# Loading the query and key weights from the ACT and GpSimd queues in a fused attention and gated-MLP layer

## The chip, the cores and the metric

The kernel runs on one core of a Trainium2 chip. The metric is the device time of one execution in microseconds. A core has five engines with one instruction stream each: TensorE (PE in the profile; its weight loads are shown as PEld), VectorE (DVE), ScalarE (ACT), GpSimd (POOL) and SyncE (SP). A copy between the chip's memory (DRAM) and the core's on-chip memory (SBUF) is an instruction on SP, ACT or POOL that hands the copy to a queue; sixteen DMA engines then move the data and report its end through a semaphore. TensorE accumulates into banks of a second on-chip memory, PSUM.

## The reference

One layer on 2048 tokens of width 512: layer norm, sliding dilated attention with 32 heads of 16 channels and 8 keys per query at distances 0, 2, ..., 14, a residual, layer norm, a gated MLP of inner width 1376, a residual. All tensors are bfloat16.

```python
x = A_x                                                # 1 x 2048 x 512
h = x + _A_ref(_layernorm(x), A_wqkv, A_wo)
h2 = h + _B_ref(_layernorm(h), B_W_gate, B_W_up, B_W_down)

def _A_ref(x, wqkv, wo):
    q, k, v = split(x @ wqkv)                          # wqkv is 512 x 1536; 32 heads of 16
    idx = pos[:, None] - arange(8) * 2                 # masked where negative
    attn = softmax(where(mask, einsum(q, k[idx]) * 16 ** -0.5, -1e9))
    return einsum(attn, v[idx]).reshape(B, S, D) @ wo

def _B_ref(x, W_gate, W_up, W_down):
    return (relu(x @ W_gate) * (x @ W_up)) @ W_down
```

## The kernel before

The 2048 tokens are worked in four chunks of 512 (tk = 0 to 3), each of four blocks of 128 rows. For a chunk, DVE takes mean and variance of each block (L419, L422), ACT forms the reciprocal root (L432, L436), DVE normalizes the block into a tile `row` (L454), and TensorE transposes it with an identity matrix (L483; for some later blocks a DMA issued from SP does it, L472). The transposed block is copied into a tile `quad` by ACT (L499) or DVE (L497). TensorE then multiplies it by the query, key and value weights (L524), each result being four matmuls, one for each quarter `dt` of the 512 input channels; ACT evicts the result (L532). DVE forms query times shifted key (L571), TensorE sums it by head (L577), ACT takes the exponential (L593), DVE weighs the values (L659) and adds up (part of the adding is an accumulating DMA issued from POOL, L691), TensorE applies the output weight (L711), and after the second layer norm come gate and up (L749), their product on DVE (L769) and down (L786).

The order of the instructions on each engine is fixed when the kernel is built. A planner replays the operations by a table of ranks, and the code emits them in that order, so the main part is the same list whatever the loads do. Ahead of it stands `setup()`, emitted in source order, which the change touches. It holds, in this order:

- the four blocks of chunk 0 of x (128 KB each), alternately on SP and ACT (L282);
- the query and key columns of wqkv as four copies of 256 KB, one for each `dt`, into `wqk_sb` (L284);
- chunk 1 of x (512 KB) on SP (L285);
- a table load on ACT (L286) and a memset on DVE for the warm-up matmuls (L287);
- on POOL: the identity matrix (masks.py lines 197 and 199), the constant `eps_t` (L289), five iotas (L290 to L294; `ci` is the first) and two memsets (L295, L296);
- a one-element copy on POOL that reads x (L299), by which the load of the value weights on SP (L300) is held until a block of x is there; and another (L301), by which the loads of chunks 2 and 3 of x (L303) are held until chunk 1 is there. The loads of `wo`, `wu`, `wg` and `wd` follow on SP (L305 to L311);
- on DVE: the constants `tmp`, `cf`, `sel`, `spread`, `same` and `mask` (L316 to L324), made from the iotas. They stand ahead of the first layer norm on DVE's list.

TensorE starts with 44 warm-up matmuls of 128 columns (L373). After the transposes of the first two blocks of chunk 0 come two sets of eight more (L381). The first query and key results of chunk 0 are computed in halves: the first half needs only the first two blocks of x, but all four quarters of `wqk_sb`. TensorE's list then goes on in this order: that half result, the four transposes of a third block, the next half result, the transposes of the fourth block, more half results.

Of the kernel before, what the change touches and what calls it, by code (L numbers as in the profile page):

```python
# [187 lines left out]
def kernel(  # L188
# [11 lines left out]
    nc = tc.nc  # L200
    Bsz, S, D = A_x.shape
# [42 lines left out]
    wqk_sb = sb.tile([P, NT, 2 * D], BF16, name="wqk_sb")  # L244
# [33 lines left out]
    def setup():  # L278

        w3_r = A_wqkv.rearrange("(dt p) f -> p dt f", p=P)  # L280
        for j in range(BPC):
            (nc.scalar if j % 2 else nc.sync).dma_start(x_sm[:, j:j + 1, :], x_rows[:, j:j + 1, :])  # L282
        for dt in range(NT):
            (nc.scalar if dt % 2 else nc.sync).dma_start(wqk_sb[:, dt:dt + 1, :], w3_r[:, dt:dt + 1, 0:2 * D])  # L284
        nc.sync.dma_start(x_sm[:, BPC:2 * BPC, :], x_rows[:, BPC:2 * BPC, :])  # L285
        nc.scalar.preload_act_table_set("natural_log_exp_and_others")  # L286
        V.memset(warm[:], 0.0)  # L287
        make_identity(nc, identity[:])
        nc.gpsimd.memset(eps_t[:], EPS)  # L289
        nc.gpsimd.iota(ci[:], pattern=[[0, 1]], base=0, channel_multiplier=1)  # L290
        nc.gpsimd.iota(sel_i[:], pattern=[[1, H]], base=0, channel_multiplier=0)
        nc.gpsimd.iota(sp_i[:], pattern=[[1, H], [0, DQ]], base=0, channel_multiplier=0)
        nc.gpsimd.iota(sm_i, pattern=[[0, 4], [1, H]], base=0, channel_multiplier=0)
        nc.gpsimd.iota(mk_i[:], pattern=[[1, PADL]], base=0, channel_multiplier=0)  # L294
        nc.gpsimd.memset(kT[:, :, 0:PADL], 0.0)  # L295
        nc.gpsimd.memset(vT[:, :, 0:PADL], 0.0)  # L296


        nc.gpsimd.tensor_copy(out=wv_sb[0:1, 0, 0:1], in_=x_sm[0:1, 0, 0:1])  # L299
        nc.sync.dma_start(wv_sb[:], w3_r[:, :, 2 * D:3 * D])  # L300
        nc.gpsimd.tensor_copy(out=x_sm[0:1, 2 * BPC, 0:1], in_=x_sm[0:1, BPC, 0:1])  # L301
        for tk in range(2, NCK):
            nc.sync.dma_start(x_sm[:, tk * BPC:(tk + 1) * BPC, :], x_rows[:, tk * BPC:(tk + 1) * BPC, :])  # L303

        nc.sync.dma_start(wo_sb[:], A_wo.rearrange("(p t) f -> p t f", t=NT))  # L305
        nc.sync.dma_start(wu_sb[:], B_W_up.rearrange("(dt p) f -> p dt f", p=P))
        nc.sync.dma_start(wg_sb[:], B_W_gate.rearrange("(dt p) f -> p dt f", p=P))
        nc.sync.dma_start(
            wd_sb[:, 0:NFF, :], B_W_down[0:NFF * P, :].rearrange("(ft p) n -> p ft n", p=P))
        if FTAIL:  # L310
            nc.sync.dma_start(wd_sb[:FTAIL, NFF, :], B_W_down[NFF * P:F, :])  # L311


        for n, (op, by) in enumerate(((ALU.arith_shift_right, 2), (ALU.bitwise_and, H - 1),
                                      (ALU.arith_shift_right, 5))):
            V.tensor_scalar(out=tmp[:, n:n + 1], in0=ci[:], scalar1=by, scalar2=None, op0=op)  # L316
        V.tensor_copy(out=cf[:, 0:3], in_=tmp[:])
        V.tensor_scalar(out=cf[:, 2:3], in0=cf[:, 2:3], scalar1=1.0 * DIL, scalar2=None, op0=ALU.mult)
        V.tensor_scalar(out=cf[:, 3:4], in0=cf[:, 2:3], scalar1=4.0 * DIL, scalar2=None, op0=ALU.add)
        V.tensor_scalar(out=sel[:], in0=sel_i[:], scalar1=cf[:, 0:1], scalar2=None, op0=ALU.is_equal)  # L320
        V.tensor_scalar(out=spread[:], in0=sp_i[:], scalar1=cf[:, 1:2], scalar2=None, op0=ALU.is_equal)
        V.tensor_scalar(out=same[:], in0=sm_i, scalar1=cf[:, 1:2], scalar2=None, op0=ALU.is_equal)
        for hf in range(2):
            V.tensor_scalar(out=mask[:, hf, :], in0=mk_i[:], scalar1=cf[:, 2 + hf:3 + hf],  # L324
                            scalar2=None, op0=ALU.is_ge)
# [488 lines left out]
    with tc.manual_schedule():  # L814
        setup()
        for op in todo:
            if op.fn is not None:
                op.fn()
# [35 lines left out]
```

## Time and profile before

| | |
|---|---|
| median of four runs | 203.56 us (203.10 to 204.19) |
| the profiled execution | 204.76 us |
| its span in the trace | 203.0 us |
| TensorE busy | 193.6 us (95% of the span) |
| DVE busy | 153.3 us (76%) |
| ACT busy | 121.8 us (60%) |
| POOL busy | 12.7 us (6%) |

The profile covers one execution. "Span" is the time from the first to the last recorded instruction; the profiled execution's own time is 1.76 us longer. Times inside the trace count from the span's start. A row such as "7.94 0.41 PE L524 MATMUL ... x2" means: from 7.94 us on, 0.41 us long, two matmuls of line 524; text in square brackets says how long the engine was idle before and what ended that. The names ACTq, SPq and POOLq stand for the sequencers that issue DMAs.

### The profile page before, as it was taken

The page shows a single profiled execution, that of the slowest core. Times are in us where ns is not written, and L with a number is a line of the kernel's source. Part 1 is how long each engine was busy: PE and PEld are TensorE (multiplying, and loading weights), DVE is VectorE, ACT ScalarE, POOL GpSimd, SP SyncE. Part 2 cuts the span into 40 slices and gives each one's busy share as a digit, 9 for nine tenths or more (in the row PEclk, how much of TensorE's full clock was granted, in tenths as well). Part 3 has the DMA queues.
Part 4 walks back from the last instruction along what each step waited for, and adds up shares of the span by engine and source line. Part 5 has one row for each costly group of instructions (what it writes and reads, how often), then busy time and mean ns, then how long its engine had stood idle before and what let it go on. Part 6 is the DMA issues. An engine that isn't in the chain of part 4 may idle for free.

```text
span 203.0 us, 2938 instructions
## 1 busy us (share of the span) xinstructions
PE 193.6 (95%) x1095; PEld 96.1 (47%) x1115; DVE 153.3 (76%) x239; ACT 121.8 (60%) x256; POOL 12.7 (6%) x28
## 2 busy tenths in 40 slices
PE   8799999989999999999999999999999999999990
PEld 8576446545445434434444444444444444444460
DVE  6689998989999999999996768799968313023241
ACT  3367698746899966787436779601567521477300
POOL 3000000420000013100131000000000000000000
PEclk9999999999999999999999999999999999999999
DMA  5969952895000009920399400221010130200103
GB/s 146 345 203 393 399 181 53 149 204 111 3 0 0 0 3 171 196 46 3 57 178 193 118 3 0 46 58 52 3 52 0 26 78 3 78 0 0 52 0 107
DMA packets 17677, 18.83 MB, mean 93 GB/s; under 512 B 8352, under 2 KB 14464, under 8 KB 17664
## 3 DMA queue, kind: packets, MB, share of 16 engines
q1 hardware_dynamic: 15360, 11.57, 18.4%
q0 software_dynamic: 1728, 6.29, 16.5%
q10 hardware_dynamic: 576, 0.79, 1.4%
q8 instruction: 9, 0.15, 0.3%
q14 instruction: 4, 0.03, 0.0%
HBM read 8.42 MB, written 2.10 MB: 52 GB/s over the span
## 4 chain that ended last, share of the span: by engine, by line
PE 65%; DVE 15%; DMA 8%; ACT 5%; SPq 2%; issue 2%; ACTq 0%
PE bank L749 28%; PE bank L524 15%; PE bank L786 14%; DVE big L659 6%; PE bank L711 5%; DMA quad<-row 4%; DMA wqk_sb<-in_A_wqkv_dram 3%; DVE big L571 3%; DVE gT L769 2%; SPq L472 1%; DVE x_sm L722 1%; DVE big L662 1%; PE bank L577 1%; PE bank L483 1%; ACT big L644 1%
## 5 line engine op out<-in xcount | busy, mean ns | idle before, releaser
L749 PE MATMUL bank<-quad,wu_sb 128*128 128x512 bf16 (+1 forms) x172 | 42.3, 379 | 0.4
L749 PE MATMUL bank<-quad,wg_sb 128*128 128x512 bf16 (+1 forms) x173 | 42.0, 379 | 0.3 <-DMA quad<-row 0.3
L756 ACT ACTIVATE gr<-bank 128x512 bf16<-128x512 f32 (+1 forms) x44 | 25.4, 618 | 24.7 <-PE bank L749 22.9
L786 PE MATMUL bank<-wd_sb,gT 128*128 128x512 bf16 (+2 forms) x183 | 39.8, 366 | 0.2
L753 ACT CAST up_sb<-bank 128x512 bf16<-128x512 f32 (+1 forms) x44 | 25.1, 601 | 21.0 <-PE bank L749 17.3
L571 DVE TENSOR_TENSOR big<-quad,kT 128x4096 bf16<-128x4096 bf16 x16 | 36.2, 2285 | 0.2
L659 DVE TENSOR_TENSOR big<-big,vT 128x4096 bf16<-128x4096 bf16 x16 | 35.9, 2281 | 0.0
L769 DVE TENSOR_TENSOR gT<-gr,up_sb 128x1024 bf16<-128x1024 bf16 (+1 forms) x24 | 15.3, 642 | 24.0 <-ACT up_sb L753 14.4
L524 PE MATMUL bank<-quad,wqk_sb 128*128 128x512 bf16 (+1 forms) x139 | 30.2, 356 | 2.0 <-DMA wqk_sb<-in_A_wqkv_dram 0.9
L786 PEld LDWEIGHTS <-gT 128*128 128x128 bf16 (+1 forms) x187 | 18.1, 98 | 19.6 <-issue 0.4
L749 PEld LDWEIGHTS <-wg_sb 128*128 128x128 bf16 (+1 forms) x176 | 17.3, 100 | 21.2 <-issue 0.9
L749 PEld LDWEIGHTS <-wu_sb 128*128 128x128 bf16 (+1 forms) x176 | 17.5, 100 | 20.6 <-issue 0.7
L524 PEld LDWEIGHTS <-wqk_sb 128*128 128x128 bf16 x144 | 15.5, 114 | 14.1 <-issue 2.4
L797 DVE TENSOR_TENSOR row<-x_sm,bank 128x512 bf16<-128x512 bf16 (+1 forms) x17 | 10.6, 649 | 10.4 <-PE bank L786 10.4
L644 ACT CAST big<-bank 128x512 bf16<-128x512 f32 x32 | 17.8, 641 | 0.4 <-PE bank L638 0.2
L662 DVE TENSOR_TENSOR big<-big 128x1024 bf16<-128x1024 bf16 (+2 forms) x24 | 16.8, 728 | 0.1
L691 POOL DMA_DIRECT2D big<-big x12 | 10.5, 872 | 87.9 <-DVE big L659 59.9
L524 PE MATMUL bank<-quad,wv_sb 128*128 128x512 bf16 x62 | 15.6, 380 | 0.2
L711 PE MATMUL bank<-wo_sb,quad 128*128 128x512 bf16 x62 | 15.2, 379 | 0.2
L454 DVE TENSOR_SCALAR row<-x_sm,mv,rs 128x512 bf16<-128x512 bf16 x32 | 11.4, 407 | 3.7 <-ACT rs L436 3.1
L499 ACT COPY quad<-bank 128x1024 bf16<-128x1024 bf16 (+1 forms) x9 | 8.0, 931 | 7.2 <-PE bank L483 7.2
L532 ACT CAST quad<-bank 128x512 bf16<-128x512 f32 x16 | 9.5, 614 | 4.6 <-PE bank L524 4.6
(68 smaller groups left out, 147.2 us busy)
## 6 DMA issues: line engine op xcount, KB each, us to landing
big<-big POOLq DMA_DIRECT2D x12, 512.0 KB, 5.5
out_dram<-row SPq DMA_DIRECT2D x15, 128.0 KB, 1.8
x_sm<-in_A_x_dram SPq DMA_DIRECT2D x3, 512.0 KB, 5.3
wu_sb<-in_B_W_up_dram SPq DMA_DIRECT2D x1, 1376.0 KB, 9.4
wg_sb<-in_B_W_gate_dram SPq DMA_DIRECT2D x1, 1376.0 KB, 12.6
wd_sb<-in_B_W_down_dram SPq DMA_DIRECT2D x1, 1280.0 KB, 15.7
wqk_sb<-in_A_wqkv_dram ACTq DMA_DIRECT2D x2, 256.0 KB, 6.5
wqk_sb<-in_A_wqkv_dram SPq DMA_DIRECT2D x2, 256.0 KB, 6.6
```

Of the source, the lines that this page charges most:

```text
L454: V.tensor_scalar(out=xn.t[:], in0=x, scalar1=mv.t[:, j, 0:1], scalar2=rs.t[:, j:j + 1], op0=ALU.add if residual else ALU.subtract, op1=AL ...
L524: nc.tensor.matmul(mm.t[:, lo:hi], lhsT=wv_sb[:, dt, t:D:NT] if c == 2 else wqk_sb[:, dt, c * D + t:(c + 1) * D:NT], rhs=xnT.t[:, dt, lo:h ...
L571: V.tensor_tensor(out=pb.t[:].rearrange("p (t w) s -> p t w s", t=2), in0=q4, in1=k4, op=ALU.mult)
L644: nc.scalar.copy(out=ab.t[:, w, :], in_=bc.t[:])
L659: V.tensor_tensor(out=mt.t[:], in0=ab.t[:], in1=v8, op=ALU.mult)
L662: V.tensor_tensor(out=mt.t[:, 0:n, :], in0=mt.t[:, 0:n, :], in1=mt.t[:, n:2 * n, :], op=ALU.add)
L711: nc.tensor.matmul(od.t[:], lhsT=OT.t[:, t, j * P:(j + 1) * P], rhs=wo_sb[:, t, :], start=(t == 0), stop=(t == NT - 1 and tk not in RPE))
L749: nc.tensor.matmul(mm.t[:fs, :], lhsT=w_sb[:, dt, ft * P: ft * P + fs], rhs=hnT.t[:, dt, :], start=(dt == 0), stop=(dt == NT - 1))
L753: nc.scalar.copy(out=ub.t[:fs, i, :], in_=um.t[:fs, :])
L756: nc.scalar.activation(out=gr.t[:fs, i, :], in_=gm.t[:fs, :], func=ACT.Relu)
L769: V.tensor_tensor(out=gt.t[:fs, 0:n, :], in0=gr.t[:fs, 0:n, :], in1=ub.t[:fs, 0:n, :], op=ALU.mult)
L786: nc.tensor.matmul(od.t[:, c0:c1], lhsT=gts[ft].t[:fs, ft % 2, j * P:(j + 1) * P], rhs=wd_sb[:fs, ft, c0:c1], start=(ft == 0), stop=(ft == ...
```

## The change

The four copies of the query and key weights are given to other queues. Before, the quarters 0 and 2 were issued by SP and 1 and 3 by ACT; after, 0 and 1 are issued by ACT and 2 and 3 by POOL.

```diff
         for dt in range(NT):
-            (nc.scalar if dt % 2 else nc.sync).dma_start(wqk_sb[:, dt:dt + 1, :], w3_r[:, dt:dt + 1, 0:2 * D])
+            (nc.scalar if dt < 2 else nc.gpsimd).dma_start(wqk_sb[:, dt:dt + 1, :], w3_r[:, dt:dt + 1, 0:2 * D])
         nc.sync.dma_start(x_sm[:, BPC:2 * BPC, :], x_rows[:, BPC:2 * BPC, :])
```

In the built program the lists of TensorE, DVE and ACT have the same instructions in the same order as before. On POOL the two copies stand ahead of the identity matrix, so ahead of all of POOL's set-up but four constant memsets. On SP the copy of chunk 1 of x follows directly on the two blocks of chunk 0.

## The prediction

> **What bounds the kernel now.** I read the page first, then the chain of waits, then the timeline of the first 11 us, then who waits for whom. The busy table puts TensorE at 95% of the span, and its clock row shows full clock all along. Where TensorE waits at all decides what a moved load can do, so I went to the start of the chain of waits (start us, length us, what):
>
> ```profile
> 2.16 7.07 DMA wqk_sb<-in_A_wqkv_dram
> 9.23 0.05 issue
> 9.28 0.41 PE bank L524 x2
> 9.69 0.22 PE bank L483 x4
> 9.91 0.44 PE bank L524 x4
> ```
>
> The reader is to see that the first thing that holds TensorE is the last of the four q/k weight copies: issued at 2.16, there at 9.23. From there the chain runs through TensorE almost without a break to 32.55. The timeline says what stands around this wait:
>
> ```profile
> 0.74 0.20 POOL masks.py:197 MEMSET identity<- 128x128 bf16 x1 [0.29 <-POOLq L838]
> 1.30 0.13 POOL L290 IOTA ci<- 128x1 int32 x1
> 1.47 0.28 DVE L316 TENSOR_SCALAR tmp<-ci 128x1 int32<-128x1 int32 x3 [0.53 <-POOL ci L290]
> 2.83 0.37 DVE L324 TENSOR_SCALAR mask<-big,cf 128x16 bf16<-128x16 int32 x2
> 3.41 0.39 SPq L285 DMA_DIRECT2D x_sm<-in_A_x_dram  x1
> 3.62 0.69 DVE L419 BATCH_NORM_STATS2 st<-x_sm 128x6 f32<-128x512 bf16 x1 [0.42 <-DMA x_sm<-in_A_x_dram]
> ...
> 6.27 0.72 PE L483 MATMUL bank<-identity,row 128*128 128x128 bf16 x8 [0.45 <-DVE row L454]
> 7.34 0.39 DVE L497 COPY quad<-bank 128x512 bf16<-128x512 bf16 x1
> 7.94 0.41 PE L524 MATMUL bank<-quad,wqk_sb 128*128 128x256 bf16 x2
> 9.28 0.41 PE L524 MATMUL bank<-quad,wqk_sb 128*128 128x256 bf16 x2 [0.93 <-DMA wqk_sb<-in_A_wqkv_dram]
> ```
>
> Here is a second chain that runs beside the weights: POOL's iota `ci` feeds DVE's constants (1.47 to 3.20), these stand ahead of the first statistics on DVE (3.62), and the layer norm of two blocks is ready for TensorE when L497 ends, at 7.34 + 0.39 = 7.73. TensorE then does half of the first group and waits 0.93 us. So weights and layer norm are both early work with little room: the layer norm has some 1.5 us before TensorE would notice, and 0.42 us of that stands at DVE's wait for x.
>
> What a copy costs on POOL is shown only later, by the accumulating copies:
>
> ```profile
> 35.78 1.01 POOL L691 DMA_DIRECT2D big<-big  x1 [25.09 <-PE bank L524]
> 37.95 0.86 POOL L691 DMA_DIRECT2D big<-big  x1 [1.17 <-DVE big L659]
> ```
>
> and the page's queue table says in how many packets copies are cut:
>
> ```profile
> q0 software_dynamic: 1728, 6.29, 16.5%
> q10 hardware_dynamic: 576, 0.79, 1.4%
> ```
>
> q10 is ACT's queue (2 x 128 KB and 2 x 256 KB, 0.79 MB), 144 packets a copy; q0 is POOL's, 1728 / 12 = 144 a copy too. One packet per row and 16 more, so a q/k copy issued from POOL should take as long to describe as an L691.
>
> **What the Trainium skill says.** "DMA: Bandwidth & Descriptors", section "Issuing engines are not separate DMA queues", says that copies from all three engines run on the same sixteen DMA engines and that spreading saves only issue time. The trace agrees that issue is small: SP and ACT spend 0.92 and 0.94 us on two weight copies that need about 7. Its section "Queues, rings and completion order" says that each DMA engine takes packets from its queues in turn; the trace shows SP's and ACT's weight copies landing 6.6 and 6.5 us after issue (medians), which fits. "Perfetto Trace Analysis", section "DMA Instruction — SWDGE (GPSIMD)", says that POOL's row ends when the last descriptor is written; so 0.86 us is taken to be POOL's own time, though no POOL compute follows an L691 closely here. "TensorE: Matmul & The Clock Gate", Part 1, says that the clock halves after an idle window of about 3.4 us; no such drop is in this trace.
>
> **The change part by part.** (1) SP loses two issues of some 0.45 us and L285 its 0.8 us wait for x (SP's waits), so chunk 1 of x is issued at 1.68 instead of 3.41. Nobody is late for chunk 1: DVE reads it at 10.48 only. The value weights behind it (L300) wait for POOL, see (3). ACT still issues two copies: nothing.
>
> (2) POOL gains two issues ahead of everything. From the L691 rows, the first 1.01 and the second 0.86: 1.87, with a gap between them 1.9 us. Bounds: 1.0 if the second is overlapped with the first, 3.0 if a copy that POOL issues cold costs half as much again. Behind them stand the identity (now needed at 6.27, ready at 1.3, so 3.2 after), `eps_t` (needed 4.63) and `ci`. DVE's constants start at 1.47 + 1.9 = 3.37 and end at 5.1, so the first statistics start at about 5.0 instead of 3.62: 1.4 late (1.9 less 0.5, the wait for x and the overlap of two DVE instructions). All of the first layer norm moves with it: the first transposes 6.27 to 7.7, L497's end 7.73 to about 9.15. TensorE then does the whole first group at once, some 0.5 us (twice the 0.25 us from 9.28 to the next transposes at 9.53): transposes at 9.65 instead of 9.53. As far as POOL goes, TensorE is 0.1 late, because the layer norm slips into the time in which TensorE waited for weights. With POOL at 3.0 it would be 1.2, with 1.0 nothing.
>
> (3) L299 on POOL moves from 3.65 to about 4.3, so the value weights are issued 0.7 later; they took 7.9 us to land and TensorE first reads them at 17.38. L301 waits for chunk 1 (10.51), which comes no later. Both cost nothing; without that cover they would cost their 0.7 us.
>
> (4) The weights themselves. Bytes ahead of the last q/k packet: x 0.52 MB and q/k 1.05 MB. The stage table gives 275 GB/s at 2 to 3 us, 379 to 3.5, then only 119 and 102 to 4.5, 209 to 5, and 324 to 367 to 9: 1.9 MB by 8.7, so 0.3 to 0.4 MB of chunk 1 went between, on DMA engines that were done with their weights. After the change chunk 1 (1 KB rows) is on SP's queue beside weights (2 KB rows) on both others, and in turns. While ACT's 16 weight packets per DMA engine pass, so do 16 of chunk 1's. A 1 KB packet at 379 / 16 = 24 GB/s is an estimated 43 ns, so 0.7 us on the DMA engine that ends last. Against that, POOL's copies start early: L691's own landing is 5.5 us after issue, and POOL's first issue moves to 0.74, 0.9 ahead of the first weight issue now. Bounds for the last landing: 8.7 (early start wins) to 10.3 (chunk 1 between, and POOL's packets also hold back x). I take 9.75, that is +0.5.
>
> TensorE goes on when both are there; it is late by the larger of 0.1 and 0.5: **+0.5 us**.
>
> (5) Does it reach the end? DVE is busy without a gap worth naming from 13.84 to 32.3 and TensorE from 9.28 to 32.5; both hang on these first transposes. The later waits on transposes and weights are relative to that work, or loads that are early (traffic falls to 11 GB/s at 28 to 33). So it passes through whole. Profiled: span 203.0 to 203.5, own time 204.76 to 205.3. The median shown is 1.2 below the profiled time, so I put the difference on the median: 203.56 + 0.5 = **204.1**.
>
> **The rivals.** About 0.5%, 1.0 us, is what a measurement here can tell from no change.
>
> A, forecast: late by 0 to 1.0 us, weights or layer norm in each other's shadow. 204.1.
>
> B, slower: POOL's two issues become the bound. Place: `ci`, then DVE's constants, then all four blocks' statistics. Price: POOL's delay less 1.8 us. It passes 1.0 from a delay of 2.8 us, 1.4 per copy against the 0.86 shown. For: the early copies are the first that POOL issues, the first L691 is longer, and POOL's spans are rough. Against: the other eleven rows agree at 0.86. At 1.8 per copy: 3.6 - 1.8 = 1.8, giving 205.4. Weights that land past 10.3 go the same way.
>
> C, slower too: the clock. TensorE's gap between warm-up (ends 5.82) and the first transposes grows from 0.45 to 1.9 us. The warm-up at 4.83 us for 44 is 110 ns each, the 16 extra ones from 6.83 take 1.06 us, 66 each: full clock is won only shortly before the layer norm arrives. If it were lost for the window that the skill names, 3.4 us of work at half speed costs 1.7 us: 205.3. Against: some 1.4 us of matmuls still fall in that window.
>
> D, faster: POOL runs on after its issue and three queues bring the weights sooner, by 8.2. Then TensorE's 0.93 us wait goes: 202.6. For: the slack between 7.73 and 9.23 is real. Against: DVE's constants are behind POOL, and the same DMA engines carry it all.
>
> E: the copies change queue and nothing else moves; 203.6, inside A's range.
>
> **How the numbers follow.** A with E 0.46, B 0.30, C 0.13, D 0.11. Of D about a fifth (0.02) stays within the bound, and of A nothing leaves it. Faster 0.09, same 0.46 + 0.02 = 0.48, slower 0.30 + 0.13 = 0.43. B weighs as much as it does because its price rests on one kind of row seen late in the trace. The range takes A's lower part with the spread of medians, 203.2, and reaches over B and C to 205.7.
>
> **What would show it.** Right: POOL's rows L284 at 0.74, `ci` at about 3.2, DVE L316 at 3.4, the first statistics at 5.0, the first transposes at 7.7, the first L524 group without a gap inside it or with a short one at 9.7, and the chain of waits starting at a q/k copy on ACT's queue. Wrong: `ci` later than 4.3 (B), matmuls of 128 columns at 110 ns each after 9 us (C), an L524 group before 9.0 (D), or a new wait past 30 us, which I have argued away.

## The result and the profile after

The changed kernel takes 205.08 us (median of 30 runs, 203.93 to 208.84) against 203.59 us before (49 runs): a ratio of 1.0074, 95% interval 1.0058 to 1.0091. It is slower by about 1.5 us. Three of its 30 executions (207.44 to 208.84 us, granted clock 0.983) are left out of the ratio, which so rests on 27. The forecast was 204.1; 205.08 lies in the upper part of the range, and the loss of 1.5 us is on the side to which 0.43 had been given.

The spans alone hide this: 203.0 before, 203.2 after. The traces differ in the last microseconds, where stores land. Compared at the last DVE instruction, the loss is there. The timeline of the kernel before, then of the changed one (start us, us, engine, line, operation, idle before it):

```profile
198.32 0.42 DVE L797 TENSOR_TENSOR row<-x_sm,bank 128x256 bf16<-128x256 bf16 x1 [0.24 <-PE bank L786]
```

```profile
199.86 0.42 DVE L797 TENSOR_TENSOR row<-x_sm,bank 128x256 bf16<-128x256 bf16 x1 [0.24 <-PE bank L786]
```

That is 1.54 us later. What follows this row took 4.3 us in the first trace of the kernel before and 2.9 in the changed one; two further traces of the kernel before (b1, b2 below) have it at 198.39 and 198.41, with 3.1 us after it. The long tail of the first trace is not repeated there.

The head of the changed kernel's trace says where the 1.54 us come from. Its timeline:

```profile
1.28 1.28 POOL L284 DMA_DIRECT2D wqk_sb<-in_A_wqkv_dram  x2 [0.83 <-POOLq L838]
1.68 0.43 SPq L285 DMA_DIRECT2D x_sm<-in_A_x_dram  x1
3.13 0.13 POOL L290 IOTA ci<- 128x1 int32 x1
3.30 0.28 DVE L316 TENSOR_SCALAR tmp<-ci 128x1 int32<-128x1 int32 x3 [2.36 <-POOL ci L290]
4.93 0.68 DVE L419 BATCH_NORM_STATS2 st<-x_sm 128x6 f32<-128x512 bf16 x1
7.58 0.72 PE L483 MATMUL bank<-identity,row 128*128 128x128 bf16 x8 [2.17 <-DVE row L454]
8.13 1.84 PE L381 MATMUL bank<-warm 128*128 128x128 bf16 x16
8.64 0.39 DVE L497 COPY quad<-bank 128x512 bf16<-128x512 bf16 x1
9.76 1.16 PE L524 MATMUL bank<-quad,wqk_sb 128*128 128x256 bf16 x4
10.09 0.35 PEld L524 LDWEIGHTS <-wqk_sb 128*128 128x128 bf16 x3 [0.28 <-DMA wqk_sb<-in_A_wqkv_dram]
10.72 0.63 PE L483 MATMUL bank<-identity,row 128*128 128x128 bf16 x4
```

Three things are to be seen. POOL's two copies push `ci` from 1.30 to 3.13, and the layer norm follows: first transposes at 7.58 instead of 6.27. The 16 extra matmuls (L381) take 1.84 us where they took 1.06: TensorE is at half speed. And the weights' wait, seen here on TensorE's weight loads (PEld), now ends at 10.09 instead of 9.23. The third block's transposes start at 10.72 instead of 9.53, 1.19 late, and by the first full-width matmuls of L524 (13.57 against 11.94 in the chains of waits) it is 1.63.

The chain of waits says which of the three this execution was held by (pieces of it, start us, length us, what):

```profile
1.28 0.53 POOL wqk_sb L284
3.17 0.10 POOL ci L290
5.02 0.61 DVE st L419
7.58 0.72 PE bank L483 x8
8.30 1.68 PE bank L381 x16
9.97 0.95 PE bank L524 x4
```

It runs from POOL's issues through `ci`, DVE and the layer norm to the matmuls at half speed. No landing of a weight copy is in it: in this execution the weights are late behind work that is later still.

The table by stages gives the clock. Columns after the stretch: its length, busy us and instructions of PE, PEld, DVE, ACT and POOL, TensorE's granted clock, DMA share, GB/s:

```profile
5.40:7.60 2.20, 0.03 (x2) 0.03 (x2) 2.13 (x7) 1.00 (x4) 0.00 (x0) 1.00 0.93 322
7.60:8.20 0.60, 0.60 (x10) 0.50 (x11) 0.60 (x3) 0.23 (x2) 0.00 (x0) 1.00 1.02 371
8.20:10.00 1.80, 1.80 (x19) 1.61 (x16) 1.51 (x5) 1.06 (x5) 0.00 (x0) 0.50 0.81 289
10.00:11.60 1.60, 1.60 (x11) 1.20 (x11) 0.21 (x1) 0.00 (x0) 0.18 (x1) 0.50 0.26 90
11.60:13.00 1.40, 1.40 (x16) 1.38 (x15) 1.40 (x4) 0.58 (x1) 0.00 (x0) 0.99 0.67 200
```

TensorE is nearly idle from 5.4 to 7.6 and then has half its clock from 8.2 to 11.6. That is rival C of the prediction, come true.

### The profile page after: what moved, and what is told of

It reads as the page before. It is cut to its first block, busy times and chain, and to the rows that moved or that the text cites. A ratio compares the mean times of both kernels' runs of the same rounds, so it can differ in the third digit from the quotient of the medians.

```text
span 203.2 us, 2937 instructions
## 1 busy us (share of the span) xinstructions
PE 194.5 (96%) x1095; PEld 97.0 (48%) x1115; DVE 153.3 (75%) x239; ACT 121.8 (60%) x256; POOL 13.8 (7%) x30
## 3 DMA queue, kind: packets, MB, share of 16 engines
q0 software_dynamic: 1888, 6.82, 17.3%
## 4 chain that ended last, share of the span: by engine, by line
PE 70%; DVE 17%; ACT 7%; issue 2%; DMA 2%; POOL 1%; ACTq 0%; POOLq 0%
PE bank L749 28%; PE bank L524 18%; PE bank L786 14%; DVE big L659 6%; PE bank L711 5%; DVE big L571 3%; DMA quad<-row 2%; DVE gT L769 2%; PE bank L483 2%; DVE x_sm L722 1%; DVE big L662 1%; PE bank L577 1%; ACT big L644 1%; ACT kT L532 1%; ACT row L408 1%
## 5 line engine op out<-in xcount | busy, mean ns | idle before, releaser
L524 PE MATMUL bank<-quad,wqk_sb 128*128 128x512 bf16 (+1 forms) x139 | 30.7, 362 | 0.9 <-ACT lnd L613 0.7
L524 PEld LDWEIGHTS <-wqk_sb 128*128 128x128 bf16 x144 | 15.9, 115 | 12.9 <-issue 2.2
L524 PE MATMUL bank<-quad,wv_sb 128*128 128x512 bf16 x62 | 15.6, 380 | 0.2
```

Of the source, the lines that this page charges most:

```text
L524: nc.tensor.matmul(mm.t[:, lo:hi], lhsT=wv_sb[:, dt, t:D:NT] if c == 2 else wqk_sb[:, dt, c * D + t:(c + 1) * D:NT], rhs=xnT.t[:, dt, lo:h ...
```

## The experiments

Three causes are to be told apart: the layer norm that POOL delays (LN), the clock that is lost in the gap this opens (CLK), and the weights' later landing (W). Nine edited kernels were run, and the two kernels again. Ratios are to the kernel before as it was timed beside each experiment, with 95% intervals. Its median there was 203.16 us beside e1 to e4, 203.52 beside e5, e7, e9 and e9b, and 203.75 beside e8; differences of medians below are to these.

An execution's mean granted clock tells whether the clock was lost on the way. One stretch of 3.41 us at half clock lowers the mean by 0.008 (half of 3.41 over a span of 203), so 0.992 or less is read as "lost", and 0.996 or more as "kept"; what is missing to 1.0 above that stands behind TensorE's last matmul. Of 120 executions of the kernel before that were timed beside the experiments, one has 0.992.

**e1: POOL's copies behind its set-up** (an edit of the changed kernel).

```diff
-            (nc.scalar if dt < 2 else nc.gpsimd).dma_start(wqk_sb[:, dt:dt + 1, :], ...)
+            if dt < 2: nc.scalar.dma_start(wqk_sb[:, dt:dt + 1, :], ...)
...
         nc.gpsimd.memset(vT[:, :, 0:PADL], 0.0)
+        [nc.gpsimd.dma_start(wqk_sb[:, dt:dt + 1, :], ...) for dt in (2, 3)]
```

> The changed kernel with POOL's two weight copies moved behind POOL's set-up (after the memset of vT), so that iota ci is back at about 1.3 us and the first statistics at 3.6. Theory LN (the layer norm is late because POOL's set-up stands behind the two issues): the loss goes, ratio to before 0.998 to 1.002. Theory W (the weights themselves land later on these queues): POOL's copies are now issued at 2.4 instead of 1.3, so the first query group waits for them until 10 us or later, ratio 1.003 to 1.007. Theory CLK (the TensorE clock is lost in the long gap before the first transposes): gap back at 0.5 us, no half clock after 8 us, ratio as in LN.

Measured: 1.0124 (1.0078 to 1.0170), slower still, and above the 1.007 expected at most. The timeline of e1:

```profile
6.15 0.72 PE L483 MATMUL bank<-identity,row 128*128 128x128 bf16 x8 [0.31 <-DVE row L454]
8.69 0.30 PE L524 MATMUL bank<-quad,wqk_sb 128*128 128x256 bf16 x1 [0.93 <-DMA wqk_sb<-in_A_wqkv_dram]
9.63 0.41 PE L524 MATMUL bank<-quad,wqk_sb 128*128 128x256 bf16 x2 [0.64 <-DMA wqk_sb<-in_A_wqkv_dram]
10.80 0.30 PE L524 MATMUL bank<-quad,wqk_sb 128*128 128x256 bf16 x1 [0.76 <-DMA wqk_sb<-in_A_wqkv_dram]
```

The layer norm is early again, and TensorE waits three times for weights, to 10.80. This execution keeps its clock, and its last DVE row is at 199.69, 1.37 us later than before. So W alone is worth nearly the whole loss when POOL's copies start 1.1 us later, and undoing LN in this way trades it for W.

Three of the six executions lose the clock all the same (0.992, at 206.09 to 207.25 us; the others take 204.79 to 205.19). The gap ahead of the first transposes is short again in e1, so LN is not the only way to lose the clock; the waits for weights are the likely other one, though no trace shows such an execution.

**e2: the kernel before, with POOL kept busy.**

```diff
         V.memset(warm[:], 0.0)
+        [nc.gpsimd.iota(sp_i[:], ...) for _ in range(4)]
```

> The kernel before, its DMAs untouched, with four extra iotas of 128x128 (0.45 to 0.55 us each) ahead of POOL's set-up, about 2 us. Theory LN with CLK: first transposes near 7.7 us instead of 6.3, half clock for 3.4 us in part of the executions, ratio 1.004 to 1.008. LN without CLK: 0.2 to 0.4 us, ratio 1.001 to 1.002. Theory W: weights land at 9.2 as before, ratio 0.999 to 1.001.

Measured: 1.0126 (1.0085 to 1.0167), above the expected 1.008. The statistics start at 5.32, 0.4 us later than in the changed kernel (4.93), so this delay is larger than the one it stands for. Five of the six timed executions show a mean granted clock of 0.983 to 0.990, the sixth 0.994. Its timeline, and a row of its table by stages:

```profile
7.96 0.75 PE L483 MATMUL bank<-identity,row 128*128 128x128 bf16 x8 [2.40 <-DVE row L454]
8.52 1.90 PE L381 MATMUL bank<-warm 128*128 128x128 bf16 x16
10.21 1.06 PE L524 MATMUL bank<-quad,wqk_sb 128*128 128x256 bf16 x4
```

```profile
8.50:10.00 1.50, 1.50 (x19) 1.50 (x17) 1.47 (x5) 1.14 (x5) 0.35 (x1) 0.51 0.91 321
```

No DMA was moved to another queue, nothing waits for weights, and the clock is lost. So LN and CLK together are enough for a loss of at least this size; what the larger delay adds was not separated.

**e3: the changed kernel, with more warm-up.**

```diff
-    NWARM, NFILL = 44, 8
+    NWARM, NFILL = 76, 8
```

> The changed kernel with 76 warm-up matmuls instead of 44, which fill TensorE's gap between 5.4 and 7.6 us. Theory CLK: no half clock after 8 us, some 0.7 to 1.0 us of the loss of 1.5 goes, ratio 1.003 to 1.004. Without CLK (the half clock is a by-product that waits hide): ratio stays at 1.006 to 1.009.

Measured: 204.34 us, 1.0057 (1.0038 to 1.0076), above the 1.004 expected at most. All 19 executions keep a clock of 0.996 or more, so the extra warm-up cures the clock. But the interval overlaps with the changed kernel's (1.0058 to 1.0091), so the size of CLK's share doesn't rest on this run; it is taken from the changed kernel's own executions below. What is left is visible in e3's timeline:

```profile
7.77 0.61 PE L483 MATMUL bank<-identity,row 128*128 128x128 bf16 x8
9.19 0.27 PE L524 MATMUL bank<-quad,wqk_sb 128*128 128x256 bf16 x1
10.33 0.52 PE L524 MATMUL bank<-quad,wqk_sb 128*128 128x256 bf16 x3 [0.86 <-DMA wqk_sb<-in_A_wqkv_dram]
```

The layer norm is ready at 9.19, as late as LN makes it, and TensorE waits for weights to 10.33.

The changed kernel's own runs give the split, since the clock is not lost in all of them. Of the 27 executions that the ratio uses, 11 have a mean granted clock of 0.996 or more and a median of 204.41 us; 16 have 0.992 or less and 205.25. So CLK adds 0.84 us where it happens (0.64 between the means), and without it the changed kernel stands 0.8 us above the kernel before. e3 stands 1.2 us above the kernel before that was timed beside it.

**e4: the changed kernel, with chunk 1 of x held back.**

```diff
-        nc.sync.dma_start(x_sm[:, BPC:2 * BPC, :], x_rows[:, BPC:2 * BPC, :])
...
+        nc.gpsimd.tensor_copy(out=x_sm[0:1, BPC, 0:1], in_=x_sm[0:1, 0, 0:1])
+        nc.sync.dma_start(x_sm[:, BPC:2 * BPC, :], x_rows[:, BPC:2 * BPC, :])
         nc.gpsimd.tensor_copy(out=wv_sb[0:1, 0, 0:1], in_=x_sm[0:1, 0, 0:1])
```

> The changed kernel with the load of chunk 1 of x held, by a one-element copy on POOL like those of the two other loads, until the first block of x is there and POOL's set-up is done (issue at about 4.4 us instead of 1.7). Theory W (chunk 1's packets go between the weights'): the weights land near 9.0 to 9.4 instead of 10.1 and the first query group runs unbroken; with the clock still lost the gain is 0.2 to 0.5 us, ratio 1.004 to 1.006. Without W: ratio as the changed kernel, 1.006 to 1.009, and the wait for weights stays.

Measured: 1.0073 (1.0045 to 1.0100), no better than the changed kernel. The hold moves two loads and not one: chunk 1 is issued at 4.44 instead of 1.68, and the value weights, which stand behind it on SP, at 4.88 instead of 4.42. So what is held back is the traffic of both. The page's table of DMA issues moved much (KB each, median us from issue to landing). The changed kernel, then e4:

```profile
wqk_sb<-in_A_wqkv_dram POOLq DMA_DIRECT2D x2, 256.0 KB, 5.5
wqk_sb<-in_A_wqkv_dram ACTq DMA_DIRECT2D x2, 256.0 KB, 7.6
```

```profile
wqk_sb<-in_A_wqkv_dram POOLq DMA_DIRECT2D x2, 256.0 KB, 4.8
wqk_sb<-in_A_wqkv_dram ACTq DMA_DIRECT2D x2, 256.0 KB, 5.8
```

ACT's copies land 1.8 us sooner, and TensorE doesn't wait for weights any more. The gain is hidden under the half clock: e4's table shows 0.51 and 0.50 from 7.9 to 11.3, and its first group starts at 10.03 behind extra matmuls of 1.91 us. Its executions divide as well: 5 with the clock kept have a median of 203.80 us, 11 without it 205.30. With chunk 1 held, no wait for weights hides part of the half clock, and it costs 1.5 us.

**e7: e3 and e4 together.** The two edits above.

> The changed kernel with chunk 1 held and 76 warm-up matmuls: layer norm still 1.3 us late behind POOL's issues, but clock kept and weights landed by 8.2. If the three named causes are all, the first query group starts at 9.2 and runs unbroken, transposes of the third block at 9.7 against 9.5 before: ratio 1.000 to 1.002. If something else is lost, 1.004 or more stays.

Measured: 203.82 us, ratio 1.0000 (0.9981 to 1.0020). Its timeline:

```profile
7.68 0.64 PE L483 MATMUL bank<-identity,row 128*128 128x128 bf16 x8
9.20 0.60 PE L524 MATMUL bank<-quad,wqk_sb 128*128 128x256 bf16 x4
9.64 0.39 PE L483 MATMUL bank<-identity,row 128*128 128x128 bf16 x4
```

With POOL's copies still first and the layer norm still some 1.3 us late, the loss is gone, to within the 0.4 us of the interval. So W and CLK account for it, and LN costs directly no more than 9.64 - 9.53 = 0.1 us in the traces. It matters by opening TensorE's gap.

**e9 and e9b: DVE's constants later.** Both emit L316 to L324 behind the fourth block's normalization, where DVE waits; e9 holds chunk 1 as well.

```diff
+    def consts():
         for n, (op, by) in enumerate(((ALU.arith_shift_right, 2), (ALU.bitwise_and, H - 1),
...
         for op in todo:
+            consts() if op.key == ("xtv3", 0) else None
```

> The changed kernel with DVE's constants emitted later as in e9 and nothing else: its DMAs are untouched. Layer norm on the old time and clock kept, so what is left is the weights alone. If they land at 10.1 to 10.3 as in the changed kernel's and e3's traces, late by 0.8 to 1.0 us: ratio 1.004 to 1.005. If the late landing there was chance, 1.000.

> The changed kernel with DVE's constants (L316 to L324) emitted behind the layer norm of the fourth block, where DVE is idle, and with chunk 1 held. POOL's copies stay first. Statistics at 3.6, first transposes at 6.3, clock kept, weights by 8.2 as in e4: the first query group 1.0 us earlier than in the kernel before, ratio 0.993 to 0.997. If weights land near 9.2 as before, 1.000.

e9b: 1.0057 (1.0032 to 1.0082), a little above the expected 1.004 to 1.005. The layer norm is back (first transposes at 6.16); against the kernel before, only the DMAs and the place of DVE's constants differ. The profiled execution, with 203.61 us nearly the fastest of its kernel, still waits:

```profile
8.27 0.30 PE L524 MATMUL bank<-quad,wqk_sb 128*128 128x256 bf16 x1 [0.50 <-DMA wqk_sb<-in_A_wqkv_dram]
9.38 0.52 PE L524 MATMUL bank<-quad,wqk_sb 128*128 128x256 bf16 x3 [0.81 <-DMA wqk_sb<-in_A_wqkv_dram]
```

15 of e9b's 22 executions keep the clock, with a median of 204.27 us, 0.75 us above the kernel before. That is W without LN and without CLK, and near the 0.8 us found above. The other seven lose the clock (0.992, 205.96 to 206.88 us) although the layer norm is early, as in e1. How late the weights landed in those no trace shows.

e9: 203.24 us, 0.9980 (0.9962 to 0.9999); expected were 0.993 to 0.997. All 22 executions keep the clock. The first group's wait ends at 8.26, and the trace ends early: the last DVE row is at 197.33 against 198.32.

**e5: POOL's copies behind its set-up and chunk 1 held** (the edits of e1 and e4).

> The changed kernel with POOL's copies behind its set-up as in e1 and chunk 1 of x held as in e4. Theory W (chunk 1's packets between the weights make them late): the weights land by 8.5 to 9.0, first query group there, ratio 0.994 to 0.999. Rival (a weight copy issued from POOL at 2.4 us is late by itself): land after 10 as in e1, ratio 1.008 or more.

Measured: 202.74 us, 0.9981 (0.9959 to 1.0003). Its timeline:

```profile
6.34 0.72 PE L483 MATMUL bank<-identity,row 128*128 128x128 bf16 x8 [1.27 <-DVE row L454]
7.94 0.60 PE L524 MATMUL bank<-quad,wqk_sb 128*128 128x256 bf16 x4
8.38 0.39 PE L483 MATMUL bank<-identity,row 128*128 128x128 bf16 x4
197.17 0.42 DVE L797 TENSOR_TENSOR row<-x_sm,bank 128x256 bf16<-128x256 bf16 x1 [0.24 <-PE bank L786]
```

This is e1 with chunk 1's load held back: there the weights made TensorE wait to 10.80, here they are in place at 7.94. A copy issued from POOL at 2.4 us is therefore not late by itself. SP's next loads, running beside the weights, make it late: chunk 1, and behind it the value weights, whose issue the hold moved from 3.86 to 4.35. The two were not held one at a time. The third block's transposes are 1.15 us earlier than in the kernel before, and all 22 executions keep the clock.

**b1 and b2, a1: the two kernels again; e8: the kernel before with chunk 1 held** (e4's edit on it).

> The kernel before once more, unchanged, for a second trace. If its weights always land as in the first trace, the first query group waits until 9.2 us. If the landing varies between executions (e2, with the same loads, shows the weights landed by 8.1), the wait is shorter here, the third block's transposes start before 9.5, and the gain of e5 and e9 over a typical execution is less than their traces' 1.1 us against the first trace.

> As b1: a third trace of the kernel before, for the spread of the weights' landing. Fixed landing: 9.2 us; varying: anything from 8.0 to 9.3.

> The changed kernel once more, for a second trace. Layer norm late by 1.3 us as before (fixed by POOL). Weights near 10 us again if chunk 1's packets are the cause; the clock is lost or kept by chance, as in a part of the timed executions.

> The kernel before, weights still on SP and ACT, with chunk 1 of x held by the one-element copy on POOL (issue near 3.9 instead of 3.4 us). Theory W in its strong form (any packet of chunk 1 ahead of the last weight costs): a small gain, ratio 0.996 to 0.999. As chunk 1 already stood behind SP's own weights, the rival is no change: 0.999 to 1.001.

b1 and b2 (203.64 and 203.65 us, one execution each) wait for weights until 9.34 and 9.24, so the first trace's landing is repeated in both. a1 (205.35 us) repeats the changed kernel: first transposes at 7.58, half clock from 8.1 to 11.5, weights to 10.50. e8 gives 0.9976 (0.9958 to 0.9994), but its trace shows nothing that would bring this: the weights' wait ends at 9.41 and the last DVE row is at 198.50. On SP chunk 1 already stood behind the weights. A ratio of 0.998 without a visible cause also says how far ratios of this size, e7's 1.0000 among them, can be trusted.

The runs side by side, with the clock kept or lost in all timed executions, and the median of those that kept it, less that of the kernel before beside them:

| kernel | layer norm late | chunk 1 held | clock kept | median of these, us |
|---|---|---|---|---|
| changed | yes | no | 11 of 30 | +0.8 |
| e3, changed with more warm-up | yes | no | 19 of 19 | +1.2 |
| e4, changed | yes | yes | 5 of 16 | +0.6 |
| e7, changed with more warm-up | yes | yes | 14 of 14 | +0.3 |
| e1, POOL's copies later | no | no | 3 of 6 | +2.0 |
| e9b, constants later | no | no | 15 of 22 | +0.8 |
| e5, POOL's copies later | no | yes | 22 of 22 | -0.8 |
| e9, constants later | no | yes | 22 of 22 | -0.3 |
| e8, loads of the kernel before | no | yes | 14 of 14 | -0.3 |

The clock is lost in part of the executions wherever the layer norm or the weights are late and the warm-up is not lengthened, and in none of these runs otherwise.

What follows for a faster version: e5 and e9 start TensorE's main work about 1 us earlier in their traces, and their ratios are 0.998, e5's with an interval that reaches above 1. As e8 shows a ratio of 0.998 without an earlier start, a gain of e5 or e9 is not settled.

## Why the prediction was right in its range and short in its size

- **The range.** 205.08 lies in it because it had been stretched over rivals B and C, to 205.7. The outcome forecast, A with a loss of at most 1.0 us, did not come. Of the 0.43 given to "slower", 0.30 stood on B, whose first road (POOL's delay) stayed shut; that side was in part right for a wrong reason.
- **What bounds the head.** Right for the kernel before: the last weight copy, in all three traces, with the layer norm as the second chain, done 1.5 us earlier. For the changed kernel the chain of waits was to start at a weight copy on ACT's queue. In its trace it starts at POOL's issues and goes through the layer norm and the half clock.
- **Part 1, chunk 1 issued at 1.68.** Right to the digit, and it was priced at nothing by itself; its effect was left to part 4.
- **Part 2, POOL.** The delay of `ci` was given as 1.9 us and is 1.83, though for other reasons: the two copies take 1.28 us of POOL together, not 1.87, but the first starts at 1.28 instead of 0.74. They are also cut in fewer packets than the 144 each that were read off the accumulating copies: the page of the changed kernel has 1888 in POOL's queue where there were 1728, so 80 each. The statistics were expected at 5.0 (4.93), the transposes at 7.7 (7.58), L497's end at 9.15 (9.03). That this costs TensorE 0.1 us directly is what e7 shows.
- **Part 3.** Nothing waited for the value weights or for chunks 2 and 3.
- **Part 4, the weights.** The mechanism was right in the main (SP's loads go between; e1, e4 and e5 show it from both sides, though with the value weights in it beside chunk 1), the term was too small: +0.5 forecast, a wait until 10.09, 10.33 and 10.50 in three traces, which is 0.9 to 1.3 later than 9.23. The early start of POOL's copies was set against it, but in the changed kernel a wait ends at the second of the four quarters, which ACT brings, and ACT's copies got slower (7.6 us against 6.5). With the clock kept, the weights cost 0.8 us in the timed runs (0.75 in e9b). Whether the packets on POOL's queue, fewer and so larger than thought, are what slowed ACT's was not tried.
- **Rival C, the clock.** This is the step that failed: it was given 0.13 and kept out of the forecast, because some 1.4 us of matmuls still fall in the window. They were about 1.2 us in the changed kernel's trace, and that was too few (the last section has the limit). The clock is lost in 16 of 27 executions. Its price was put at 1.7 us; it is 0.84 in the changed kernel, where the wait for weights runs under it, and 1.5 in e4, where it doesn't.
- **Rival B.** POOL's delay never came near the 2.8 us from which it was to cost 1.0. Its other road, weights that land past 10.3, is touched by 10.33 in e3 and 10.50 in a1. Rival D did not occur, but its opening was real: in e5 TensorE's wait for the weights is gone.
- **Part 5, passing through.** Right: 1.19 at the third block's transposes, 1.63 at 13.57, 1.54 at the end.

The loss divided by measured terms: 0.82 for the weights (204.41 - 203.59), and 0.84 x 16 / 27 = 0.50 for the clock, 1.3 us of the 1.5. Both terms are taken from the runs that also give the loss, so this divides it and does not check it. The check on the first is e9b.

## What to carry to other kernels

Moving a load to another queue also moves everything behind it on the old queue: here SP's next loads came forward and took the place in the traffic that the weights had left. A queue that computes passes the cost of an issue on to whatever its set-up feeds, and a delay that is free on paper can still open a gap on TensorE long enough to cost it its clock; so count TensorE's idle time in the warm-up before calling a delay hidden. And compare two traces at the last compute instruction, not by their spans, when the difference is one microsecond.

## What the hardware showed that was not expected

- TensorE's granted clock changes in steps of 3.41 us in these traces. The changed kernel's goes to 1.0 at 4.79, to 0.5 at 8.20 and back at 11.62; e2's at 5.10, 8.52 and 11.93. In the stretch ahead of the drop TensorE was busy for about 1.2 of 3.41 us (0.6 of warm-up and 0.6 from 7.58 on); in the kernel before, with about 2.2 us of work in the stretch from 5.64, the clock was kept. The Trainium skill, "TensorE: Matmul & The Clock Gate", Part 1, gives the window as about 3.4 us, and the trace agrees; where it speaks of an idle window, these traces show a drop after a window that was one third busy.
- The fourteen traces together give a limit. Cut into such stretches from the first rise of the clock on, every stretch at full clock in which TensorE's matmul rows fill 0.40 or less (18 of them, at the head of the kernel and at its end) is followed by half the clock, and every one in which they fill 0.44 or more (787) is not. To win the clock took more: counted back from the first rise, a stretch filled to 0.66 in e9 was not followed by full clock, one filled to 0.90 in e5 was.
- The steps do not start with the kernel. The first rise comes anywhere from 4.07 (e5) to 6.67 us (e9), so the same gap can fall within one stretch or be shared by two. This is the likely reason why the changed kernel loses its clock in a part of its executions only; it was not tested.
- The weight copies take POOL less time, 1.28 us for two, than the accumulating ones (0.86 each), but the first began 0.54 us later than POOL's first memset after the constants had. What POOL does in that half microsecond no row shows.
- In e2, with the kernel before's loads, the weights landed 4.9 to 5.9 us after issue instead of 6.1 to 7.1. Its value weights were issued at 4.80 instead of 3.92; whether that is the reason was not tried.
